# A fused attention and Fourier kernel on one Trainium2 core: most big loads past the thirteenth product issued by ScalarE in place of SyncE

## The chip, the core and the metric

The kernel runs on one core of a Trainium2 chip. The core has five engines that run their own instruction streams and wait for each other by semaphores: TensorE (PE, matrix products into PSUM banks), VectorE (DVE), ScalarE (ACT), GpSimd (POOL) and SyncE (SP, which computes nothing and here issues DMAs). Sixteen DMA engines move data between HBM and on-chip memory; an instruction on SP, ACT or POOL starts a transfer. The metric is device time in microseconds of one execution, lower is better.

## What is computed

Two independent parts, put side by side in the output. Part A is causal sliding-window attention with 32 heads of 32 columns and a window of 256; part B is a two-dimensional Fourier transform written as products with given matrices, of which the real part is kept.

```python
# A: x, wqkv, wo of 2048x1024, 1024x3072, 1024x1024
qkv = x @ wqkv
scores = einsum("bhqd,bhkd->bhqk", q, k) * (Dh ** -0.5)
scores = where((i - j >= 0) & (i - j < 256), scores, -1e9)
a = einsum("bhqk,bhkd->bhqd", softmax(scores), v) @ wo
# B: x of 2048x1024, matrices of 2048x2048 and 1024x1024
re, im = x @ dft_hid_re.T, x @ dft_hid_im.T
b = dft_seq_re @ re - dft_seq_im @ im
out = concatenate([a, b], axis=-1)
```

Everything is float32 in and out.

## The kernel before

**Products.** Each float32 operand is scaled and split into a high and a low float16 half (`split`, L129: ACT writes the high half, DVE the low one); three passes of float16 matmuls (`PASSES`, L48) replace one float32 product. The time runs through three stages.

*First stage* (L948 to L985, to about 560 us): 96 products of 24 matmuls with 512 columns each, listed in `order` (L409): q, k and v of eight head groups. The three PSUM banks of `bank` rotate; `qk_out` (L905) and L968 to L975 copy a finished bank by ACT (L907, L968) and DVE (L126, L969), and SP stores the result to the scratch tensors `qk` and `vs` in HBM. `tasks` (L414) ties other work to the number n of a product: loads, maxima or means (`top`, `mean`), scales and splits of later weights, and the preparation of part B: `xp_load` and `xp_step` (L631, L636) turn blocks of B's x into seven sums for a Strassen-like product and store them in `xs`; `wp_load` and `wp_step` (L668, L676) do so for the hidden-dimension matrices in the tile `wx` (views `praw(0)` to `praw(3)`).

*Rounds* (L1121 to L1202, to about 1540 us): 48 units in four rounds of 12. A round has four units of kind x (hidden transform) and eight of kind c (sequence transform). A unit is one call of `seven` (L1047): seven products of 12 matmuls, at positions 0 to 6, into the banks a, b, a, c, a, b, a. After position 0 ACT copies bank a into bank c (L1084), after positions 1, 2, 3 and 6 it copies a bank to an output tile (L1053), after 4 and 5 DVE adds (L1055). A bank is used again after one other product, so a copy has about one product's time. After each position, `hook(n, turn)` runs what `do(n, turn, ...)` noted for it: `u_load` loads the two float32 halves of a coming unit of kind c from `cs` into `raw_u` (five buffers `raw`), `u_top` takes their mean on ACT, `u_scale` makes the scale (a small product `pt_u` on PE), `u_step` splits them into `un_a`, `un_b`, `un_c`. For a unit of kind x, `x_left` loads these from `xs` instead.

*Attention* (`attention`, L218) is woven into both stages: `tick` (L382) advances it after every few matmuls by a rate. A block b has the scores of 128 queries for two heads (PE `s` and `far`), a mask copy and maximum (DVE), exponentials (ACT L278), a split (ACT L281, DVE L282), a transposing DMA on SP (L284) and two masks on POOL; six blocks later comes the product with v. `do_load` (L226) fetches q and k of four blocks into one of two `qk` buffers, three blocks ahead of use (L370) or, where the data isn't there yet, at use (L249).

*Last stage* (L1205 on): the product with wo.

**Order.** A scheduler places instructions on each engine from the program's order and its own estimate of times. `tc.issue_after(x)` only forbids a place ahead of x. Each engine runs its stream strictly in order. `behind_act[0]` is the last ACT copy of a bank. Tiles come from pools with a fixed number of buffers; a load into a buffer waits until its last reader is done. Each DMA on SP or ACT reports on one of eight completion semaphores, taken in turn, and waits for the DMA that used the same one before.

Before the change SP issues every transfer but the stores that accumulate (POOL, L1145): loads, transposes and stores stand in one stream.

Of the kernel before, what the change touches and what calls it, by code (L numbers as in the profile page):

```python
# [15 lines left out]
AF = mybir.ActivationFunctionType  # L16
# [29 lines left out]
HP = 8 * P  # L46
# [7 lines left out]
def fused_kernel(ctx: ExitStack, tc: tile.TileContext, xa, wqk, wv, wo, xb, wd, cs, out):  # L54
    nc = tc.nc
    PSUM = bass.MemoryType.PSUM

    qk = tc.dram_tile((NG, NCH, 3, DH, HG, 2, CH), F16, name="qk")
# [42 lines left out]
    nbank, units_on, stored, soon = [0], [], [], [True]  # L101
# [4 lines left out]

    def load_raw(src, shape, name, pool=None, tag="raw", **kw):
        r = (pool or rawp).tile([P] + shape, F32, tag=tag, name=f"raw_{name}", **kw)
        with tc.issue_after(stored[0].ins) if stored else nullcontext():
            nc.sync.dma_start(r, src)  # L110
        return r


# [31 lines left out]

    behind = []

    marks = []

    def top(key, raw, i, n):  # L150

        if i == 0:
            tops[key] = small.tile([P, n], F32, tag=f"top{n}", name=f"top_{key}")
        with tc.issue_after(behind[0].ins) if behind else nullcontext():
            vec(nc.vector.tensor_reduce, tops[key][:, i:i + 1], raw, axis=AX.XY, op=ALU.max,
                apply_absolute_value=True)

    def mean(key, raw, i, n):

# [58 lines left out]
    def attention():  # L218
# [4 lines left out]
        st, cur, q2s, k2s, vts, store_o = {}, {}, {}, {}, {}, []  # L223
        far = ps_s.tile([P, 2, 2, P], F32, tag="far", bufs=1, name="far")

        def do_load(g, hp, sc):  # L226
            if (g, hp, sc) in q2s:
                return
            u = att.tile([96, 2, 2, CH], F16, tag="qk", name=f"qk_{g}_{hp}_{sc}")
            nc.sync.dma_start(u.rearrange("p h a t -> p (h a t)"), qk[g, sc, :, :, 2 * hp:2 * hp + 2]  # L230
                              .rearrange("j d h a t -> (j d) (h a t)"))
            q2s[g, hp, sc], k2s[g, hp, sc] = u[:, :, 0], u[:, :, 1]

        def do_load_v(g, hp, sc):
# [8 lines left out]
        def s_step(b, j):  # L243
            g, hp, sc, i = blocks[b]
            qb = sc * QB + i
            nb = min(qb + 1, 3)
            if j == 0:
                if i == 0:
                    do_load(g, hp, sc)  # L249
                    do_load_v(g, hp, sc)  # L250
                st[b] = {"s": ps_s.tile([P, 2, 2 * P], F32, tag="s", name=f"s_{b}")}
                if nb == 3:
                    st[b]["far"] = far[:, b % 2]
            d = st[b]
            s = d["s"]
            edges = [k for k in range(qb + 1 - nb, qb + 2) if k in (qb + 1 - nb, qb - 1, qb + 1) or k % QB == 0]
            for k0, k1 in zip(edges, edges[1:]):
                at = (k0 - (qb - 1)) * P
                mm(d["far"][:, j] if at < 0 else s[:, j, at:at + (k1 - k0) * P],
                   q2s[g, hp, sc][:, j, i * P:i * P + P],  # L260
                   k2s[g, hp, k0 // QB][:, j, k0 % QB * P:k0 % QB * P + (k1 - k0) * P],
                   start=True, stop=True, skip_group_check=True)
            if j == 0:
                return
            w = min(nb, 2) * P
            sv = s[:, :, 2 * P - w:]
            nc.vector.copy_predicated(s[:, :, P:], upper2, d["far"] if nb == 3 else never2)  # L267
            mx = att.tile([P, 2], F32, tag="mn", bufs=6, name=f"mx_{b}")
            nc.vector.tensor_reduce(mx, sv, axis=AX.X, op=ALU.max, negate=True)  # L269
            bias = att.tile([P, 3], F32, tag="bias", bufs=6, name=f"bias_{b}")  # L270
            es = esc[g][:, sc:sc + 1]
            nc.scalar.activation(bias[:, :2], mx, AF.Identity, bias=pshift, scale=es)  # L272
            if b % 2 == 1:

                marks[:] = [nc.gpsimd.tensor_scalar(bias[:, 2:3], bias[:, 0:1], 1.0, None, op0=ALU.mult)]  # L275

            for h in range(2):
                nc.scalar.activation(sv[:, h], sv[:, h], AF.Exp, bias=bias[:, h:h + 1], scale=es)  # L278
            hl = att.tile([P, 8 * P], F16, tag="hl", bufs=3, name=f"hl_{b}")
            hi, lo = (hl[:, a * w:a * w + 2 * w].rearrange("p (h k) -> p h k", h=2) for a in (0, 2))  # L280
            nc.scalar.activation(hi, sv, AF.Copy)  # L281
            behind[:] = [nc.vector.tensor_tensor(lo, sv, hi, op=ALU.subtract)]  # L282
            t = att.tile([P, 8, P], F16, tag="t", bufs=6, name=f"t_{b}")
            line[:] = [nc.sync.dma_start_transpose(t[:, :4 * min(nb, 2)], hl[:, :4 * w])]  # L284
            d["t"] = t
# [66 lines left out]
        for b in range(nblk + LAG):  # L352
            for j in range(2):
                yield (blocks[b][0], blocks[b][2]) if b < nblk else None
                if b < nblk and j == 0:
                    s_step(b, 0)
                    s_step(b, 1)
                if j == 1 and b % 2 == 0 and b >= LAG:
                    v_step(b - LAG)
                    g, hp, sc, i = blocks[b - LAG + 1]  # L360
                    if i == QB - 1:
                        o_step(g, hp, sc)
                if j == 1 and b % 2 == ZAT and 3 <= b < nblk + 4:
                    for m in (b - 3 - (ZAT == 0), b - 2 - (ZAT == 0)):
                        if 0 <= m < nblk:
                            z_step(m)
                if j == 1 and store_o and (b >= nblk or blocks[b][3] == 3):
                    with tc.issue_after(line[0].ins):
                        nc.sync.dma_start(*store_o.pop(0))
                if j == 1 and b < nblk and blocks[b][3] == 1 and b + 3 < nblk:  # L370
                    g, hp, sc, _ = blocks[b + 3]
                    if (g, sc) in ready:
                        do_load(g, hp, sc)
                if j == 1 and b < nblk and blocks[b][3] == 3 and b + 1 < nblk:
                    g, hp, sc, _ = blocks[b + 1]
                    if (g, sc) in ready:
                        do_load_v(g, hp, sc)
# [78 lines left out]
    def praw(i):  # L456
        return cellx["wx"][:, i * 2048:(i + 1) * 2048].bitcast(F32)
# [106 lines left out]
    behind_act = []  # L564
# [66 lines left out]
    def xp_load(m):  # L631
        c, k = m // 4, m % 4
        for j, t in ((0, 8 * c + k + 4), (1, 8 * c + k)):
            nc.sync.dma_start(praw(m % 2 * 2 + j), xb[t].rearrange("p d t -> p (d t)"))

    def xp_step(n, m, step):  # L636
        r1, r2 = (praw(m % 2 * 2 + j).rearrange("p (d t) -> p d t", t=P) for j in range(2))
# [30 lines left out]
    def wp_load(p, k, blocks):  # L668
        for b in blocks:
            src = wd[p, 1 - b % 2, 2 * (b // 2) + k]  # L670
            if p == 1:
                nc.sync.dma_start(praw(b), src.rearrange("p d c -> p (d c)"))
            else:
                held[k, b] = load_raw(src, [2, CH], f"wd{k}_{b}")

# [97 lines left out]
    def u_load(n, j=0):  # L773
        if n < len(units):
            kind, p, c, i = units[n]
            raws[n, j] = rawp.tile([P, ND, P], F32, tag="raw", name=f"raw_u{n}_{j}")
            (load if i < 2 else nc.sync.dma_start)(raws[n, j], cs[p, 2 * i + j, :, 8 * c:8 * c + 8])

    def u_top(n, j):

# [17 lines left out]
    def x_left(n, step):  # L798

        _, _, c, k = units[n]  # L800
        src = xs[4 * c + k]
        u = uns.setdefault(n, {})
        part = lambda t, k0: (lambda h, d: t[:, h, k0 + d])
        if step == "t":
            t = spare[:, k % 2 * 8 * P:(k % 2 + 1) * 8 * P]
            nc.sync.dma_start(t, src[:, 6 * HP:])
            u[5] = part(t.rearrange("p (h k t) -> p h k t", h=2, k=4), 0)
            return
        j, held_by = {"a": (0, (0, 3)), "c": (1, (6, 4)), "b": (2, (2, 1))}[step]
        t = stp.tile([P, 2, ND, P], F16, tag="st", name=f"un{n}_{step}").rearrange("p h d t -> p (h d t)")  # L810
        nc.sync.dma_start(t, src[:, 2 * j * HP:2 * (j + 1) * HP])
        for k, pos in enumerate(held_by):
            u[pos] = part(t[:, k * HP:(k + 1) * HP].rearrange("p (h d t) -> p h d t", h=2, d=4), 0)

# [291 lines left out]
    with tc.tile_pool(name="pb", bufs=1) as pb:  # L1106
# [11 lines left out]
        def do(n, turn, f, *args):  # L1118
            todo.setdefault((n, turn), []).append((f, args))

        for r in range(4):  # L1121
# [7 lines left out]
                    do(n - 1, 0, x_left, n, "t")  # L1129
            for j in range(8):  # L1130
                n = c0 + j
                do(n - 3, 1, u_load, n, 1)
                do(n - 3, 5, u_load, n, 0)
                do(n - 2, 0, u_top, n, 1)
                do(n - 2, 2, u_top, n, 0)
                do(n - 2, 6, u_scale, n)
                for step, turn in enumerate((0, 1, 1, 2, 3, 4)):
                    do(n - 1, turn, u_step, n, step)
# [125 lines left out]
```

## Time and profile before

| What | Value |
|---|---|
| runs | 1696.62, 1700.10, 1697.67 us; median 1697.67 |
| profiled execution | 1697.51 us, span 1695.7 us |
| HBM read, written | 166.99 MB, 106.17 MB |
| hardware DMA queue q1 | 321.48 MB, 75.9% of 16 engines |
| granted TensorE clock | 1.000 |

The median issue-to-landing times of the loads that matter are 4.8 us (`raw_u` and `qk`), 4.8 to 5.5 us (`un_a`, `un_b`, `un_c`), 5.6 us (`raw_wd`), 5.9 us (`xb` into `wx`).

Rows of the timeline give the start and duration in us, the engine (SPq is SP's instruction stream, PEld PE's weight loads), the line of the kernel, the operation, output<-inputs by tile name, shapes and a count; in brackets, the engine's idle time ahead and what ended it. A row of waits gives who waited for whom: total us, times, longest us. Matmul ends are modelled, and adjacent matmuls overlap in the records.

### The profile page before, as it was taken

How to read it: one execution, taken by the hardware profiler on the slowest of the kernel's cores; microseconds unless marked ns; L12 is line 12 of the kernel's file. 1: busy time of each engine (PE TensorE's matmuls, PEld its weight loads, DVE VectorE, ACT ScalarE, POOL GpSimd, SP SyncE). 2: the span in 40 equal slices, each digit the busy share in tenths (PEclk: the TensorE clock that was granted, in tenths of full speed). 3: DMA queues.
4: the chain of work that ended last, by engine and by line, in shares of the span. 5: the costliest groups of instructions: out<-in, count | busy, mean ns of one | idle time of the engine just before them, and what ended most of it. 6: DMA issues, size and time to landing. Idle time of an engine off the chain costs nothing.

```text
span 1695.7 us, 30919 instructions
## 1 busy us (share of the span) xinstructions
PE 1687.6 (100%) x11007; PEld 846.6 (50%) x11007; DVE 1304.8 (77%) x2256; ACT 1169.8 (69%) x2035; POOL 571.0 (34%) x812
## 2 busy tenths in 40 slices
PE   9999999999999999999999999999999999999999
PEld 4444545554555554555554555545555545444444
DVE  7657888888888689887688896688886698687442
ACT  4476666677877687887687886687887688563322
POOL 0000222334434341444423475433565425411000
DMA  6678999999999994887998999986999977866431
GB/s 246 239 269 246 248 289 285 279 259 303 245 234 222 208 225 122 205 200 171 232 245 250 196 182 182 230 200 120 193 183 203 227 181 140 174 184 120 116 99 75
DMA packets 469898, 348.62 MB, mean 206 GB/s; under 512 B 376944, under 2 KB 409968, under 8 KB 468848
## 3 DMA queue, kind: packets, MB, share of 16 engines
q1 hardware_dynamic: 462064, 321.48, 75.9%
q0 software_dynamic: 7680, 25.17, 9.0%
q8 instruction: 86, 1.41, 0.3%
q14 instruction: 68, 0.56, 0.1%
HBM read 166.99 MB, written 106.17 MB: 161 GB/s over the span
## 4 chain that ended last, share of the span: by engine, by line
PE 83%; ACT 4%; DMA 4%; DVE 3%; issue 3%; POOL 2%; SPq 0%; POOLq 0%; ACTq 0%; DVEq 0%
PE p_a L119 23%; PE pv L119 12%; PE p_b L119 11%; PE pk L119 9%; PE pq L119 9%; PE p_c L119 6%; PE po_a L119 5%; PE s L119 3%; PE po_b L119 2%; PE far L119 1%; PE po_c L119 1%; DMA o<-ohl 1%; POOL z L296 1%; ACT s L278 1%; POOL t L298 1%
## 5 line engine op out<-in xcount | busy, mean ns | idle before, releaser
L278 ACT ACTIVATE s<-s,bias,escs 128x256 f32<-128x256 f32 (+1 forms) x512 | 270.1, 528 | 11.7
L296 POOL TENSOR_SCALAR_AFFINE_SELECT z<-t 128x512 f16<-128x512 f16 x224 | 183.1, 825 | 190.0 <-PE pv L119 167.2
L275 POOL TENSOR_SCALAR bias<-bias 128x1 f32<-128x1 f32 x128 | 53.5, 418 | 548.0 <-ACT bias L272 405.3
L272 ACT ACTIVATE bias<-mx,pshift,escs 128x2 f32<-128x2 f32 x256 | 98.4, 384 | 165.4 <-DVE mx L269 164.4
L282 DVE TENSOR_TENSOR hl<-s,hl 128x512 f16<-128x512 f32 (+1 forms) x256 | 169.8, 664 | 50.4 <-ACT hl L281 49.9
L119 PEld LDWEIGHTS <-reg 128*128 128x128 f16 x1344 | 128.7, 97 | 141.6
L298 POOL TENSOR_SCALAR_AFFINE_SELECT t<-t 128x512 f16<-128x512 f16 x224 | 188.1, 848 | 11.6
L119 PE MATMUL p_a<-reg,un_c 128*128 128x512 f16 x768 | 181.4, 379 | 0.5 <-DVE reg L859 0.3
L119 PE MATMUL pk<-reg,wu_k 128*128 128x512 f16 x768 | 174.3, 379 | 0.0
L269 DVE TENSOR_REDUCE mx<-s 128x2 f32<-128x512 f32 (+1 forms) x256 | 170.7, 667 | 3.4
L119 PE MATMUL pv<-reg,reg 128*128 128x512 f16 x768 | 172.5, 379 | 0.0
L119 PEld LDWEIGHTS <-un_c 128*128 128x128 f16 x1152 | 109.9, 97 | 121.8 <-issue 2.4
L119 PEld LDWEIGHTS <-un_b 128*128 128x128 f16 x1152 | 109.4, 97 | 117.4 <-issue 0.7
L119 PEld LDWEIGHTS <-un_a 128*128 128x128 f16 x1152 | 109.4, 97 | 116.5
L119 PE MATMUL pq<-reg,wu_q 128*128 128x512 f16 x696 | 156.3, 379 | 0.0
L281 ACT ACTIVATE hl<-s 128x512 f16<-128x512 f32 (+1 forms) x256 | 148.8, 581 | 5.5
L119 PE MATMUL p_a<-reg,un_b 128*128 128x512 f16 x576 | 136.4, 379 | 0.1
L119 PE MATMUL p_c<-reg,un_a 128*128 128x512 f16 x576 | 136.5, 379 | 0.0
L119 PE MATMUL p_b<-reg,un_b 128*128 128x512 f16 x576 | 136.3, 379 | 0.1
L119 PE MATMUL p_a<-reg,un_a 128*128 128x512 f16 x576 | 136.2, 379 | 0.0
L267 DVE COPY_PREDICATED s<-upper,far 128x256 f32<-128x256 uint32 x224 | 94.3, 421 | 51.6 <-PE s L119 50.6
L119 PEld LDWEIGHTS <-qk 96*128 96x128 f16 x1056 | 87.6, 97 | 63.6 <-DMA qk<-qk 2.2
(217 smaller groups left out, 3136.6 us busy)
## 6 DMA issues: line engine op xcount, KB each, us to landing
raw_u<-in_cs_dram SPq DMA_DIRECT2D x64, 512.0 KB, 4.8
qk<-qk SPq DMA_DIRECT2D x64, 384.0 KB, 4.8
out_dram<-y POOLq DMA_DIRECT2D x72, 256.0 KB, 6.2
raw_wd<-in_wd_dram SPq DMA_DIRECT2D x24, 512.0 KB, 5.6
vs<-yv SPq DMA_DIRECT2D x32, 264.0 KB, 4.1
vt<-vs SPq DMA_DIRECT2D x64, 132.0 KB, 3.5
qk<-yq SPq DMA_DIRECT2D x32, 256.0 KB, 4.0
raw_wo<-in_wo_dram SPq DMA_DIRECT2D x16, 512.0 KB, 8.6
```

The costliest lines, as they stand in the source:

```text
L119: fixed[:] = [nc.tensor.matmul(*args, **kwargs)]
L267: nc.vector.copy_predicated(s[:, :, P:], upper2, d["far"] if nb == 3 else never2)
L269: nc.vector.tensor_reduce(mx, sv, axis=AX.X, op=ALU.max, negate=True)
L272: nc.scalar.activation(bias[:, :2], mx, AF.Identity, bias=pshift, scale=es)
L275: marks[:] = [nc.gpsimd.tensor_scalar(bias[:, 2:3], bias[:, 0:1], 1.0, None, op0=ALU.mult)]
L278: nc.scalar.activation(sv[:, h], sv[:, h], AF.Exp, bias=bias[:, h:h + 1], scale=es)
L281: nc.scalar.activation(hi, sv, AF.Copy)
L282: behind[:] = [nc.vector.tensor_tensor(lo, sv, hi, op=ALU.subtract)]
L296: nc.gpsimd.affine_select(out=z, in_=pk, compare_op=ALU.is_gt, fill=0.0, base=0, pattern=[[0, 4], [-1, P]], channel_multiplier=1)
L298: nc.gpsimd.affine_select(out=pk, in_=pk, compare_op=ALU.is_ge, fill=0.0, base=0, pattern=[[0, 4], [1, P]], channel_multiplier=-1)
```

## The change

Loads issued by ACT get a helper, `bulk`, with a place behind the last copy of a bank by ACT. `load_raw` uses it once product 12 has been reached (`soon` is then False). So do the loads of `xb` and of `wd` into `wx`, `u_load` and `x_left`. The prefetch of `qk` three blocks ahead moves to ACT as well, with a place behind the exponentials of the block before the present one (`behind_exp`); the load at use stays on SP. `u_load` and `u_top` come one turn later. Transposes, stores, value tiles (`vt`), the loads of wo and of attention results for the last stage and the four `w_slot` loads to reg2 and three to wx stay on SP.

```diff
     def load_raw(src, shape, name, pool=None, tag="raw", **kw):
         r = (pool or rawp).tile([P] + shape, F32, tag=tag, name=f"raw_{name}", **kw)
-        with tc.issue_after(stored[0].ins) if stored else nullcontext():
-            nc.sync.dma_start(r, src)
+        if soon[0]:
+            with tc.issue_after(stored[0].ins) if stored else nullcontext():
+                nc.sync.dma_start(r, src)
+        else:
+            bulk(r, src)
         return r
...
-    marks = []
+    marks, behind_exp = [], []
...
+    def bulk(dst, src):
+        with tc.issue_after(behind_act[0].ins) if behind_act else nullcontext():
+            nc.scalar.dma_start(dst, src)
...
-        def do_load(g, hp, sc):
+        def do_load(g, hp, sc, queue=None):
...
-            nc.sync.dma_start(u.rearrange("p h a t -> p (h a t)"), qk[g, sc, :, :, 2 * hp:2 * hp + 2]
-                              .rearrange("j d h a t -> (j d) (h a t)"))
+            with tc.issue_after(behind_exp[0].ins) if queue else nullcontext():
+                (queue or nc.sync).dma_start(u.rearrange("p h a t -> p (h a t)"), qk[g, sc, :, :, 2 * hp:2 * hp + 2]
+                                             .rearrange("j d h a t -> (j d) (h a t)"))
...
-                nc.scalar.activation(sv[:, h], sv[:, h], AF.Exp, bias=bias[:, h:h + 1], scale=es)
+                e = nc.scalar.activation(sv[:, h], sv[:, h], AF.Exp, bias=bias[:, h:h + 1], scale=es)
+            behind_exp[:] = behind_exp[-1:] + [e]
...
                     if (g, sc) in ready:
-                        do_load(g, hp, sc)
+                        do_load(g, hp, sc, nc.scalar)
...
-            nc.sync.dma_start(praw(m % 2 * 2 + j), xb[t].rearrange("p d t -> p (d t)"))
+            bulk(praw(m % 2 * 2 + j), xb[t].rearrange("p d t -> p (d t)"))
...
             if p == 1:
-                nc.sync.dma_start(praw(b), src.rearrange("p d c -> p (d c)"))
+                bulk(praw(b), src.rearrange("p d c -> p (d c)"))
...
-            (load if i < 2 else nc.sync.dma_start)(raws[n, j], cs[p, 2 * i + j, :, 8 * c:8 * c + 8])
+            bulk(raws[n, j], cs[p, 2 * i + j, :, 8 * c:8 * c + 8])
...
-            nc.sync.dma_start(t, src[:, 6 * HP:])
+            bulk(t, src[:, 6 * HP:])
...
-        nc.sync.dma_start(t, src[:, 2 * j * HP:2 * (j + 1) * HP])
+        bulk(t, src[:, 2 * j * HP:2 * (j + 1) * HP])
...
-                do(n - 3, 1, u_load, n, 1)
-                do(n - 3, 5, u_load, n, 0)
-                do(n - 2, 0, u_top, n, 1)
-                do(n - 2, 2, u_top, n, 0)
+                do(n - 3, 2, u_load, n, 1)
+                do(n - 3, 6, u_load, n, 0)
+                do(n - 2, 1, u_top, n, 1)
+                do(n - 2, 3, u_top, n, 0)
```

SP's DMA rows fall from 1127 to 870 and ACT gets 257. Line numbers of the changed kernel are larger by 3 to 9 (L1053 becomes L1062, L786 becomes L795); all loads through `bulk` carry L163 there. PE keeps its instructions; only small products for scales (`pt`) move. Three places, in the built order:

SP before, in the first stage at product 67, ahead of the load `qk_1_1_0` (group 1, second pair of heads); `yq4_3` and `yk4_0` are results of products on their way to HBM:

```order
L284 DMA_TRANSPOSE t_44_4283<-hl_44_4280 128x8x128
L349 DMA_TRANSPOSE o_1_0_1_4155<-ohl_1_0_1_4322 128x4x128
L911 DMA qk_57<-yq4_3_4340 128x2x512
L912 DMA qk_57<-yq4_3_4340 128x512
L230 DMA qk_1_1_0_4395<-qk_57 96x2048
L912 DMA qk_57<-yk4_0_4422 128x512
```

ACT after the change, at the same place:

```order
L290 ACTIVATE hl_44_4280<-s_44_4266 128x512
L355 ACTIVATE ohl_1_0_1_4322<-o_1_0_1_4155 128x256
L916 ACTIVATE yq4_3_4340<-pq4_3_4257 128x512
L170 ACTIVATE junk_100,top_wq5_4345<-raw_wq5_4192 128x1024
L163 DMA wx_113<-in_wd_dram 128x1024 x2
L238 DMA qk_1_1_0_4395<-qk_57 96x2048
L280 ACTIVATE bias_45_4377<-mx_45_4375,pshift_95,escs_118 128x2
L286 ACTIVATE s_45_4369<-s_45_4369,bias_45_4377,escs_118 128x256 x2
```

The load no longer stands behind the two stores of `yq4_3`, but behind the ACT copy that makes `yq4_3`, a mean and two other loads, and ahead of block 45's exponentials.

SP before, in the rounds between units 20 and 21 (`t_169` to `t_173` are transposes of attention blocks, `raw_u23_0` a half of unit 23):

```order
L777 DMA raw_u23_0_12500<-in_cs_dram 128x1024
L284 DMA_TRANSPOSE t_169_12404<-hl_169_12401 128x8x128
L284 DMA_TRANSPOSE t_170_12443<-hl_170_12440 128x8x128
L284 DMA_TRANSPOSE t_171_12522<-hl_171_12519 128x8x128
L369 DMA ots_59<-o_5_0_0_12206 128x512
L240 DMA vt_5_0_3_12533<-vs_58 128x4x132
L284 DMA_TRANSPOSE t_172_12572<-hl_172_12569 128x8x128
L349 DMA_TRANSPOSE o_5_0_1_12459<-ohl_5_0_1_12622 128x4x128
L230 DMA qk_5_1_0_12684<-qk_57 96x2048
```

ACT after the change, from the last copy of unit 20 (`y1<-p2_20_a`) on:

```order
L1062 ACTIVATE y1_6683<-p2_20_a_12261,sc_u20_11939 128x512
L163 DMA raw_u23_0_12541<-in_cs_dram 128x1024
L280 ACTIVATE bias_171_12512<-mx_171_12510,pshift_95,escs_118 128x2
L286 ACTIVATE s_171_12504<-s_171_12504,bias_171_12512,escs_118 128x256 x2
L135 ACTIVATE un22_a_12579<-raw_u22_0_12258,sc_u22_12534 128x1024
L290 ACTIVATE hl_171_12517<-s_171_12504 128x512
L1093 ACTIVATE p2_21_c_12546<-p2_21_a_12544 128x512
```

The load now stands behind the copy of position 6. The mean of `raw_u23_1`, which stood there before, comes twelve rows later, behind the copy of position 1.

ACT before, in the first stage at the first products of v (`xp1` is the mean of two blocks of B's x in `wx`):

```order
L968 ACTIVATE yv0_1_1028<-pv0_1_1003,vf_105 128x16x32
L163 ACTIVATE junk_100,top_wo_551<-raw_wo_6_994 128x1024
L132 ACTIVATE wx_113<-wx_113,vxp_106 128x512
L968 ACTIVATE yv0_2_1071<-pv0_2_1046,vf_105 128x16x32
L163 ACTIVATE junk_100,top_xp1_1082<-wx_113 128x1024 x2
```

and after:

```order
L977 ACTIVATE yv0_1_1028<-pv0_1_1003,vf_105 128x16x32
L170 ACTIVATE junk_100,top_wo_551<-raw_wo_6_994 128x1024
L135 ACTIVATE wx_113<-wx_113,vxp_106 128x512
L163 DMA wx_113<-in_xb_dram 128x1024 x2
L977 ACTIVATE yv0_2_1071<-pv0_2_1046,vf_105 128x16x32
L163 DMA raw_wd1_0_1076<-in_wd_dram 128x1024
L170 ACTIVATE junk_100,top_xp1_1082<-wx_113 128x1024 x2
```

The two loads for `xp1` stand one bank copy ahead of the instruction that reads them; on SP they had been issued at 88.7 and 94.1 us, some 40 us ahead of it.

## Prediction

> **What bounds the kernel now.** I read the page's busy line first, then busy time by stretch, then the waits of TensorE. In the stretch table the columns are: stretch and length, then busy microseconds of PE, its weight loads, DVE, ACT and POOL with instruction counts, granted clock, DMA share and GB/s.
>
> ```profile
> span 1695.7 us, 30919 instructions
> PE 1687.6 (100%) x11007; PEld 846.6 (50%) x11007; DVE 1304.8 (77%) x2256; ACT 1169.8 (69%) x2035; POOL 571.0 (34%) x812
> ...
> 80.00:340.00 260.00, 260.00 (x1593) 128.22 (x1592) 199.32 (x384) 179.18 (x304) 54.60 (x85) 1.00 0.94 272
> 340.00:560.00 220.00, 218.48 (x1609) 114.00 (x1605) 182.78 (x321) 163.39 (x288) 90.03 (x128) 1.00 1.01 250
> 560.00:600.00 40.00, 39.62 (x308) 21.05 (x306) 28.53 (x49) 29.06 (x57) 16.37 (x26) 1.00 1.03 208
> 600.00:1130.00 530.00, 529.31 (x3792) 273.71 (x3791) 432.80 (x771) 417.20 (x767) 227.56 (x323) 1.00 0.91 205
> 1130.00:1500.00 370.00, 369.66 (x2507) 187.31 (x2506) 295.97 (x518) 277.14 (x490) 171.22 (x226) 1.00 0.89 183
> ```
>
> The change acts from about 77 us to 1500 us. Between 80 and 1500 us PE lacks 0 + 1.52 + 0.38 + 0.69 + 0.34 = 2.93 us. The clock is granted in full. "Busy" alone could deceive, since a record of a 512-column matmul overlaps the next; so I checked the spacing of starts.
>
> ```profile
> 880.94 2.75 PE L119 MATMUL p_b<-reg,un_b 128*128 128x512 f16 x12
> 883.15 0.55 ACT L1084 ACTIVATE p_c<-p_a 128x512 f32<-128x512 f32 x1
> 883.75 2.75 PE L119 MATMUL p_a<-reg,un_b 128*128 128x512 f16 x12
> ```
>
> Twelve matmuls whose modelled ends span 2.75 us are 2.59 us of work by their starts (the chain of waits writes the same groups as 2.59), 0.216 us each. The last record outlives its slot by 0.16 us, so a wait is up to 0.16 us longer than PE's idle time says. These are PE's waits after 5 us:
>
> ```profile
> PE s L119 <- DMA qk<-qk: 1.5, 1, 1.5
> ...
> PE p_a L119 <- ACT y L1053: 0.4, 1, 0.4
> PE p_a L119 <- DVE y L1055: 0.3, 1, 0.3
> PE p_a L119 <- DVE reg L859: 0.3, 1, 0.3
> PE p_a L119 <- ACT p_c L1084: 0.2, 1, 0.2
> ```
>
> Five waits: 2.93 + 5 x 0.16 = 3.7 us is all that the change can win, and it can win that only by doing everything right. 3.4 us (0.2%) is about what a measurement of this kernel can tell from no change. So the question is what the change can lose.
>
> **The change part by part.** It issues 257 loads from ACT instead of SP: 64 `raw_u`, 64 pieces from `xs`, 60 `qk`, 24 blocks from `xb` and `wd` into `wx`, 24 `raw_wd`, and 21 others (6 wo, 4 wv, 7 wk, 4 wq). What one issue takes, from the views of two source lines (min/median/max in ns):
>
> ```profile
> L777 SPq DMA_DIRECT2D raw_u<-in_cs_dram x48: 327/338/1226, 629.3 to 1487.9; - x48
> ...
> L230 SPq DMA_DIRECT2D qk<-qk x64: 319/498/1600, 122.6 to 1415.4; - x64
> ```
>
> At 0.34 to 0.50 us, 257 issues are some 110 us of SP's time that become ACT's. No row shows ACT issuing a DMA. Bounds: nothing, if ACT's sequencer issues while the engine still works; 0.45 us each, if the engine stands. The nearest rows lean to the first:
>
> ```profile
> 1007.57 0.60 ACT L281 ACTIVATE hl<-s 128x512 f16<-128x512 f32 x1
> 1008.06 0.68 ACT L1053 ACTIVATE y<-p_b,sc_u 128x512 f32<-128x512 f32 x1
> ```
>
> Each begins 0.11 us before the one ahead ends, so the sequencer is ahead of the engine, and a moved load mostly stands behind a copy of 0.6 to 0.7 us that can cover 0.34 to 0.50.
>
> *What an uncovered issue costs.* In the rounds ACT copies finished banks (L1084, L1053), and PE comes back to a bank one product later. At 883.15 + 0.55 = 883.70 the copy ends, 0.05 us before PE needs it; elsewhere there is 2.08 us:
>
> ```profile
> 1004.86 0.56 ACT L1084 ACTIVATE p_c<-p_a 128x512 f32<-128x512 f32 x1
> ...
> 1007.50 1.03 PE L119 MATMUL p_a<-reg,un_c 128*128 128x512 f16 x4
> ...
> 595.69 0.68 ACT L1053 ACTIVATE y<-p_a,fx 128x512 f32<-128x512 f32 x1
> ...
> 1497.35 0.58 ACT L1084 ACTIVATE p_c<-p_a 128x512 f32<-128x512 f32 x1
> ```
>
> Reading each such pair, 13 copies leave under 0.5 us (the first and last are the last two rows); their slack adds up to 2.4 us. A full 0.45 us in front of each costs 13 x 0.45 - 2.4 = 3.4 us, a covered one nothing. I take the middle, +1.7 us: cover is the rule, but not every issue stands ahead of a tight copy nor behind a long instruction.
>
> *What it wins.* The one large wait of PE:
>
> ```profile
> 393.92 1.05 ACT L163 ACTIVATE junk<-raw_wq 128x1024 uint8<-128x1024 f32 x1
> ...
> 404.30 0.39 SPq L230 DMA_DIRECT2D qk<-qk  x1
> ...
> 408.87 0.28 PE L119 MATMUL s<-qk 96*128 96x128 f16 x2 [1.52 <-DMA qk<-qk]
> ```
>
> The load stands on SP behind transposes and the stores of `yq4_3`. On ACT it stands behind the mean of `wq5`, which ends at 394.97. PE wanted it at 408.87 - 1.52 = 407.35; it takes 4.57 us from issue to first use, so anything ahead of 402.8 will do. -1.5 us. What is late next is the other qk load of that stretch, which no listed wait names.
>
> *Waits that move along.* SP had waited for buffers on behalf of these loads:
>
> ```profile
> SPq L777 <- DVE un_c L126: 33.4, 13, 4.1
> SPq L777 <- DVE un_b L126: 20.9, 13, 2.3
> SPq L811 <- PE s L119: 15.0, 12, 2.5
> SPq L806 <- PE p_b L119: 13.8, 9, 4.4
> ```
>
> If ACT waited for them, exponentials and bank copies would queue behind. But SP waited because it was early:
>
> ```profile
> 998.14 1.27 DVE L126 SCALAR_TENSOR_TENSOR un_b<-raw_u,sc_u,un_b 128x1024 f16<-128x1024 f32 x1
> ...
> 999.37 0.54 SPq L777 DMA_DIRECT2D raw_u<-in_cs_dram  x1
> ...
> 1001.46 0.69 ACT L1053 ACTIVATE y<-p_a,sc_u 128x512 f32<-128x512 f32 x1 [1.05 <-PE p_a L119]
> ```
>
> SP issues as DVE frees the buffer; the new place is behind the copy at 1001.46, 2 us after that. For `qk` it is the same: its buffer is freed by the scores of the block at hand, and the exponentials next in line on ACT need those scores too. New is that a load on ACT can stand for a DMA of SP: all loads, stores and transposes share eight completion semaphores in turn, and each waits for the one eight back. Eight back is some 12 us at about 1,130 DMAs in 1,696 us, against landings of 4 to 6 us. I cost these waits at nothing; uncovered, they are the second rival. Transposes and stores come sooner on SP, which has 257 rows fewer; PE waits for none of them, so nothing. POOL keeps its instructions, but for seven pairs of neighbours that change places.
>
> Sum: 1697.5 (profiled execution: span 1695.7 and 1.8 around it; the median is 1697.67) - 1.5 + 1.7 = **1697.7 us**, no change that can be told.
>
> **The rivals.** *Issue is held up by transposes (slower).* The large transposes alone keep SP issuing for 256 x 1.25 = 320 us, a fifth of the span, and an issue right behind one is long:
>
> ```profile
> L284 SPq DMA_TRANSPOSE t<-hl x256: 1188/1254/6185, 147.1 to 1453.5; - x128
> ...
> 1014.10 1.25 SPq L349 DMA_TRANSPOSE o<-ohl  x1
> 1015.45 1.60 SPq L230 DMA_DIRECT2D qk<-qk  x1
> ```
>
> If ACT's issues suffer the same, a fifth of some 170 in the rounds are 1.1 us longer than the median, which no 0.7 us copy covers. At one tight copy in five and 0.5 us each that is 34 x 0.2 x 0.5 = 3.4 us, with the 3.4 of the 13 places: 1697.5 - 1.5 + 6.8 = 1702.8. It decides the sign once more than about 5 us of ACT delay reach PE. Against it: the 1.60 can be a full queue of SP alone.
>
> *The waits come along (much slower).* The four rows are 83 us in 47 waits, 1.8 us each. ACT's idle time from 600 to 1500 us is 112.8 + 92.9 = 206 us; 83 of waits and 77 of issues would use 160 of it. If half of the waits meet a copy with 1 us of slack, 23 x 0.8 = 18 us: about 1716. The Trainium skill, page "DMA: Bandwidth & Descriptors", section "Anatomy of one DMA", says that DMA engines never wait for semaphores, the issuing sequencer does so ahead of dispatch; by that rule whatever is not yet free stops ACT. The rows above say that it is free.
>
> *Loads land late.* Issued where ACT stands, loads lose SP's head start. In the first stage the pair for `xp1` now stands behind the copy of `yv0_1` and a split, some 3.5 us ahead of its mean:
>
> ```profile
> wx<-in_xb_dram SPq DMA_DIRECT2D x16, 512.0 KB, 5.9
> ...
> 128.02 0.71 ACT L132 ACTIVATE wx<-wx,vxp 128x512 f16<-128x512 f32 x1
> 132.21 1.05 ACT L163 ACTIVATE junk<-wx 128x1024 uint8<-128x1024 f32 x1
> ```
>
> A landing time of 5.9 us makes ACT stand for about 2.4 us there, and at some dozen like places. A product takes 24 x 0.216 = 5.2 us and three banks rotate, so copies have 10 us and PE sees nothing unless stands add up: +4 us if they do at two or three places, 1701.5. The Trainium skill, page "DMA: Bandwidth & Descriptors", section "Queues, rings and completion order", has each DMA engine take turns between SP's row of queues and ACT's, packet by packet: loads would then share the engines with transposes that now stand behind them, and by that rule land later still. This profile has one hardware queue and shows neither.
>
> *All of PE's waits vanish (faster)*: 1697.5 - 3.7 = 1693.8.
>
> **How the numbers follow.** Forecast 0.60, transposes 0.17, late loads 0.10, waits along 0.06, faster 0.07. Faster by over 0.2% 0.07, within 0.60, slower 0.33. The range is 1694.2 to 1706.5: below it is most of the faster case, above it the waits-along case and the upper part of the first rival, together under 0.2. The likeliest case alone spans 1694.3 to 1701.
>
> **What would show it.** A second hardware queue on the page; no wait of PE for `qk` near 407; SP's waits on `un_b` and `un_c` gone and no ACT wait of their size in their place. Right: PE's waits for L1084 and L1053 together under 4 us. Wrong: those rows at 5 us and more with issues of over 1 us on ACT ahead of the copies (first rival), ACT issues that wait for DVE or PE (second), or ACT's means waiting for DMA with PE idle before 350 us (third).

## The result and the profile after

| | before | after |
|---|---|---|
| median of 4 runs | 1698.88 us (1696.62 to 1704.37) | 1812.63 us (1786.46 to 1834.74) |
| profiled execution | 1697.51 us, span 1695.7 | 1786.46 us, span 1784.7 |
| ratio to before | 1 | 1.0554, 95% interval 1.0467 to 1.0641 |

The change makes the kernel about 5.5% slower. The runs of the changed kernel spread over 2.7%; the ratio is that of the runs within 1.5% of the fastest on either side, so it lies below the ratio of the medians, and the profile is of the fastest run, so it shows the least of the damage.

The page of the changed kernel first: the busy line of PE and the DMA queues (packets, MB, share of 16 engines).

```profile
span 1784.7 us, 30812 instructions
...
PE 1710.0 (96%) x11007; PEld 850.3 (48%) x11007; DVE 1301.5 (73%) x2256; ACT 1170.4 (66%) x2035; POOL 557.9 (31%) x812
...
q1 hardware_dynamic: 426976, 198.78, 54.5%
q10 hardware_dynamic: 35088, 122.70, 25.4%
```

ACT and DVE have no more work than before (ACT 1170.4 against 1169.8 us, DVE 1301.5 against 1304.8), and the same 321.48 MB are moved, but 122.70 MB of them go through a second hardware queue, q10. PE has the same 11007 instructions; its records last 22 us longer in all, and it is idle for 75 - 8 = 67 us more. Busy time by stretch, columns as in the prediction:

```profile
80.00:340.00 260.00, 247.66 (x1475) 120.22 (x1474) 178.62 (x342) 167.67 (x284) 46.49 (x75) 0.99 0.92 241
340.00:560.00 220.00, 203.04 (x1443) 103.80 (x1442) 171.29 (x311) 147.86 (x260) 81.44 (x113) 0.98 1.10 247
...
600.00:1130.00 530.00, 511.84 (x3644) 262.98 (x3642) 413.25 (x736) 399.71 (x732) 209.52 (x308) 0.99 0.97 193
1130.00:1500.00 370.00, 348.03 (x2383) 176.56 (x2382) 282.37 (x490) 266.21 (x484) 150.69 (x211) 0.98 0.95 173
```

PE lacks 12.3, 17.0, 18.2 and 22.0 us in stretches where it lacked 0, 1.5, 0.7 and 0.3, and the clock is no longer granted in full. What PE waits for (total us, times, longest):

```profile
PE far L122 <- DVE s L275: 22.0, 14, 3.8
PE p_a L122 <- ACT p_c L1093: 16.2, 6, 10.2
PE p_a L122 <- ACT y L1062: 7.2, 9, 2.0
PE pv L122 <- DVE yv L978: 4.3, 2, 3.2
PE pv L122 <- POOL z L305: 4.0, 2, 3.4
PE p_b L122 <- DMA un_b<-xs: 3.1, 1, 3.1
...
PE s L122 <- DMA qk<-qk: 0.7, 1, 0.7
```

Hardly any of it is for a load. PE waits for DVE's mask copies and ACT's bank copies, so ACT and DVE are late. DVE waits for ACT in its turn, most of all for ACT's write of the high half into `hl`, here after the change and then before it.

```profile
DVE hl L291 <- ACT hl L290: 116.5, 66, 12.7
```

```profile
DVE hl L282 <- ACT hl L281: 49.9, 56, 2.7
```

Why ACT is late is seen in the source lines that issue on ACT, and in the transposes of the tile `hl` (issue times in ns, min/median/max; then who waited for it, us and times):

```profile
L163 ACTq DMA_DIRECT2D raw_u<-in_cs_dram x64: 334/335/394, 633.0 to 1581.4; - x64
...
L238 ACTq DMA_DIRECT2D qk<-qk x60: 310/333/411, 216.3 to 1504.2; - x60
```

```profile
L293 SPq DMA_TRANSPOSE t<-hl x256: 1194/1443/11602, 148.4 to 1540.3; - x128
...
  POOL z L305: 111.1, 31
  ACT hl L290: 40.1, 12
  ACT s L286: 14.9, 2
...
DMA to landing us min/median/max: 3.0/6.2/26.0
```

The same view of the kernel before ends:

```profile
  POOL z L296: 22.5, 11
  ACT yk L907: 1.8, 1
...
DMA to landing us min/median/max: 2.4/4.6/13.0
```

Issuing on ACT is cheap, 0.33 us at the median and never over 0.42 in these two rows; of all 257 loads one takes more than 1 us to issue (1.45 us). The transposes, which the change does not touch, are what became slow: from 4.6 to 6.2 us at the median, from 13.0 to 26.0 at most, and by my count of the trace 47 of 256 land after more than 10 us where 2 did. They meet more loads the longer they take: in the changed kernel's trace a transpose (of `hl` or `ohl`) lands after 3.66 us (median of 35) when no load of ACT overlaps it, 4.49 with one (79), 6.08 with two (82), 8.38 with three (59), 11.15 with five (23). This alone does not say which is the cause, since a transpose that is late for any reason overlaps more loads; the experiments have to.

The largest hole, as the timeline has it: SP first, then ACT, then PE.

```profile
1378.28 19.38 SPq L293 DMA_TRANSPOSE t<-hl  x3
...
1386.14 0.33 ACTq L163 DMA_DIRECT2D un_a<-xs  x1
1386.72 0.38 ACT L280 ACTIVATE bias<-mx,pshift,escs 128x2 f32<-128x2 f32 x1
1399.85 0.33 ACTq L163 DMA_DIRECT2D reg<-xs  x1
1400.23 1.11 ACT L286 ACTIVATE s<-s,bias,escs 128x256 f32<-128x256 f32 x2 [13.13 <-DMA t<-hl]
1401.37 0.60 ACT L290 ACTIVATE hl<-s 128x512 f16<-128x512 f32 x1
1401.86 0.59 ACT L1093 ACTIVATE p_c<-p_a 128x512 f32<-128x512 f32 x1
...
1402.51 1.44 PE L122 MATMUL p_a<-reg,un_b 128*128 128x512 f16 x3 [10.23 <-ACT p_c L1093]
```

Loads of `un_a`, `un_b`, `un_c` are in flight and three transposes take 19.4 us to issue. The next load in ACT's order, `reg<-xs`, takes its turn on a completion semaphore that a transpose used last; it stands until that transpose lands, 12.8 us. Exponentials and the bank copy L1093 stand behind it, and PE stands for the copy. The price does not end there (stretch, length, busy PE to POOL, granted clock):

```profile
1393.00:1402.00 9.00, 0.00 (x0) 0.00 (x0) 0.00 (x1) 1.71 (x4) 1.86 (x3) 0.65 1.14 236
1402.50:1405.50 3.00, 3.00 (x8) 1.04 (x8) 1.22 (x3) 2.03 (x5) 1.91 (x4) 0.50 0.87 197
1406.00:1409.40 3.40, 3.40 (x20) 1.67 (x19) 1.81 (x3) 1.14 (x3) 1.53 (x3) 1.00 1.02 155
```

After the hole PE runs at half its clock for another 3 us: 8 matmuls of 512 columns, where at 0.216 us each 13 would fit. Over the whole trace the clock is halved for 41 us, in seven pieces behind holes. Taking PE's spacing of starts against that of before, 48 holes of over 0.3 us make 77.8 us and 74 matmuls at half clock another 14.6. With the 4.6 us of before taken off that is 87.8 of the 89 us between the two spans.

### The profile page after: what moved, and what is told of

Read it like the earlier page. It is cut to its first block, busy times and chain, and to the rows that moved or that the text cites. A ratio compares the mean times of both kernels' runs of the same rounds, so it can differ in the third digit from the quotient of the medians.

```text
span 1784.7 us, 30812 instructions
## 1 busy us (share of the span) xinstructions
PE 1710.0 (96%) x11007; PEld 850.3 (48%) x11007; DVE 1301.5 (73%) x2256; ACT 1170.4 (66%) x2035; POOL 557.9 (31%) x812
## 3 DMA queue, kind: packets, MB, share of 16 engines
q10 hardware_dynamic: 35088, 122.70, 25.4%
q0 software_dynamic: 7680, 25.17, 9.2%
## 4 chain that ended last, share of the span: by engine, by line
PE 61%; DMA 16%; DVE 9%; ACT 8%; issue 4%; POOL 1%; SPq 1%; ACTq 0%; DVEq 0%; POOLq 0%
PE p_a L122 18%; PE pq L122 9%; PE p_b L122 9%; DMA t<-hl 7%; PE pv L122 6%; PE p_c L122 5%; PE po_a L122 4%; PE pk L122 4%; PE po_b L122 2%; ACT s L286 2%; PE s L122 2%; DMA xs<-wx 2%; DMA wx<-in_xb_dram 1%; PE po_c L122 1%; DMA raw_wd<-in_wd_dram 1%
## 5 line engine op out<-in xcount | busy, mean ns | idle before, releaser
L305 POOL TENSOR_SCALAR_AFFINE_SELECT z<-t 128x512 f16<-128x512 f16 x224 | 176.9, 797 | 233.3 <-PE pv L122 111.3
L283 POOL TENSOR_SCALAR bias<-bias 128x1 f32<-128x1 f32 x128 | 45.7, 357 | 591.5 <-ACT bias L280 419.4
L290 ACT ACTIVATE hl<-s 128x512 f16<-128x512 f32 (+1 forms) x256 | 148.7, 582 | 50.0 <-DMA t<-hl 40.1
L122 PE MATMUL pv<-reg,reg 128*128 128x512 f16 x768 | 176.1, 384 | 4.3 <-DVE yv L978 4.3
L122 PE MATMUL p_a<-reg,un_b 128*128 128x512 f16 x576 | 140.6, 387 | 16.2 <-ACT p_c L1093 14.9
```

Of the source, the lines that this page charges most:

```text
L122: fixed[:] = [nc.tensor.matmul(*args, **kwargs)]
L305: nc.gpsimd.affine_select(out=z, in_=pk, compare_op=ALU.is_gt, fill=0.0, base=0, pattern=[[0, 4], [-1, P]], channel_multiplier=1)
```

## The experiments

Three theories were set against each other. **Turns**: two hardware queues share the DMA engines, and transposes on SP's queue land late behind loads of ACT's. **Standing**: ACT, strictly in order, stands at its loads for shared semaphores and for their issue. **Late places**: the loads are asked for too late, whoever asks. Differences in us below are of medians, to the runs of before beside them.

**The same places, issued by SP.**

```diff
-            nc.scalar.dma_start(dst, src)
+            nc.sync.dma_start(dst, src)
...
-                        do_load(g, hp, sc, nc.scalar)
+                        do_load(g, hp, sc, nc.sync)
```

> The changed kernel with its 257 loads at the same places of the program (behind the last bank copy or the exponentials, means one turn later), but issued by SP again: one hardware queue. Turns theory (two hardware queues share the DMA engines packet by packet, so that transposes on SP's queue land late behind loads of ACT's queue, and hold ACT and POOL): the loss goes, 1696 to 1706 us, landing of t<-hl at 4.6 us median and 13 at most. Standing theory (ACT, strictly in order, stands at its loads for completion semaphores that it shares with SP): the loss goes too, same range. Late-places theory (the loads are asked for too late, whichever engine asks): the loss stays, 1770 us and above.

1706.97 us against 1699.44, ratio 1.0047 (1.0029 to 1.0065). The landing of its `t<-hl`:

```profile
DMA to landing us min/median/max: 2.4/4.9/11.6
```

The places cost 7.5 us, 1 us above the range of turns and standing; the rest of the loss needs another queue or another issuer. Late places falls as the main cause.

**ACT issues, but moves nothing.** The kernel before, and beside each of the 257 loads:

```diff
+    def tiny(after=None):
+        after = behind_act if after is None else after
+        ntiny[0] += 1
+        with tc.issue_after(after[0].ins) if after else nullcontext():
+            nc.scalar.dma_start(tinies[ntiny[0] % 16], cs[0, 0, :1, 0])
```

> The kernel before, with all loads on SP, and beside each of the 257 loads a copy of 512 bytes from HBM to HBM that ACT issues at the place where the change puts the load. These take completion semaphores in turn with SP's transfers, and ACT must issue them in order, but they move next to nothing. Turns theory: no traffic on the second queue, so 1696 to 1703 us, t<-hl landing at 4.6 us median. Standing theory (shared semaphores and issue): most of the loss stays, 1760 us and above, with ACT's copies waiting several us for transposes. Late-places theory: 1696 to 1703.

1711.03 us, ratio 1.0066 (1.0046 to 1.0086): 11.6 us, above the range of turns and far below that of standing. In its trace ACT stands for 24.5 us, 16 times, at one of these copies whose semaphore a transfer of SP used last. So standing is real, and with the issue itself, and with transposes that land as before (4.6 us at the median), it is worth an eighth of the loss (11.6 of 94 us). What standing costs when the transposes are late, this run does not show.

**Smaller packets.** The changed kernel, with rows of 4 KB cut in HBM to rows of 1 KB; the control is the kernel before with the same layout.

```diff
-    xs = tc.dram_tile((8, P, 7 * HP), F16, name="xs")
+    xs = tc.dram_tile((8, 14, P, HP // 2), F16, name="xs")
...
-            nc.scalar.dma_start(dst, src)
+            nc.scalar.dma_start(cut(dst), rows(src))
...
+    wqk, wv, wo, xb, wd, cs = (cut(m) for m in (wqk, wv, wo, xb, wd, cs))
```

> The changed kernel with the inputs (all but xa) and the scratch tensor xs laid out in HBM so that a row of 4 KB becomes four of 1 KB: loads move the same bytes from the same places on ACT, in packets of 1 KB in place of 4 KB (qk loads keep 4 KB). Turns theory: a 256-byte packet of a transpose waits for one packet of the other queue per turn; 64 of them per DMA engine, behind packets of about 46 ns in place of about 160 ns, wait some 3 us and not up to 10: t<-hl landing at most 15 us in place of 26, and at least half of the loss goes, 1700 to 1745 us. Standing and late-places theories: packet size means nothing or costs a little, 1780 us and above.

> Control: the kernel before, all on SP, with the same HBM layout in rows of 1 KB. All theories: 1696 to 1706 us; if it is slower than that, the difference is the price of smaller packets and is taken off the run with small packets on ACT.

The control: 1706.24 us, ratio 1.0036 (1.0022 to 1.0051). With ACT's loads: 1769.88 us (1749.62 to 1787.67), ratio 1.0320 (1.0275 to 1.0365). Less the control's 0.36%, about half of the 5.54% is left, so packet size matters, which standing and late places do not explain. But the time is above the range given, and in the one profile, of a run of 1787.67 us, a transpose still takes 24.1 us to land, 37 of 256 take more than 10 us, and the median landing is 6.1 us, against 6.2. The most direct measure is the rate of the transposes' 256-byte packets, counted in the trace in slices of 0.5 us between 90 and 1500 us:

| kernel | second queue still, packets per us | second queue moving |
|---|---|---|
| changed, rows of 4 KB | 655 | 250 |
| rows of 1 KB | 674 | 299 |
| rows of 512 bytes (below) | 675 | 364 |

The levels depend on which slices are counted, the order less so: over all slices that lie between two with transposes, the rates are 535, 520 and 541 with the second queue still and 214, 245 and 306 with it moving.

**Rows of 512 bytes, and the changed kernel again.**

> As the run with rows of 1 KB, but with rows of 512 bytes. If the queues take turns by packets, the transposes get a still larger share: their rate while the second queue is moving rises well over the 299 packets per us of the run with 1 KB (250 with 4 KB), and the time falls to 1715 to 1750 us. If the share is not by packets, the rate stays near 300 and the time at 1750 to 1790 us, or rises, as smaller packets take more time of the DMA engines for the same bytes.

> The changed kernel once more, on the same chip as the two others: 1785 to 1835 us by all theories, t<-hl landing at a median of about 6.2 us. It says whether single profiles of it can be compared with those of the variants.

With 512 bytes 1765.18 us (1761.09 to 1784.24), ratio 1.0412 (1.0354 to 1.0470); the changed kernel again 1820.48 us (1803.63 to 1834.38). The rate rose as turns by packets has it, and the longest landing fell to 15.0 us. The time is not below that of 1 KB and lies in the range given for the other case; the median landing is 6.3 us, and 30 transposes still take more than 10 us. The second queue's share of the DMA engines also rose, from 25.4 to 28.6%, and rows of 512 bytes have no control on one queue. So smaller packets take some of the loss away, and the runs don't settle how much of it; that the queues take turns by packets agrees with the rates and is not shown by the times.

**One part of the loads at a time.** All three keep the places of the change; the parts not named are issued by SP.

> The changed kernel in which only the 69 loads of the first stage (weights, scans, blocks of xb and wd) are issued by ACT; the 128 loads of the rounds and the 60 qk prefetches go back to SP, at the same places. Turns theory: the loss comes where loads of the second queue meet transposes, so PE's holes lie before 560 us, t<-hl lands late there alone (over 10 us at most a dozen times after 560), 1725 to 1745 us. Standing theory (each issue on ACT costs, about 94 us over 257 loads): 69 loads cost some 25 us, 1732 us, but t<-hl lands no later than before.

> The changed kernel in which only the 128 loads of the rounds (raw_u, pieces of xs) are issued by ACT, the others by SP at the same places. Turns theory: PE's holes lie after 560 us, t<-hl lands late there (median over 5.5 us in the rounds), 1725 to 1750 us. Standing theory: 128 of 257 loads, some 47 us, 1754 us, with t<-hl landing as before.

> The changed kernel in which only the 60 qk prefetches are issued by ACT, the others by SP at the same places. Turns theory: a single load of 384 KB at a time adds at most about 1 us to a transpose, so 1703 to 1712 us, hardly more than with all loads on SP at these places (1707.0). Standing theory: 60 loads of 257, some 22 us on top of 1707, 1729 us.

| loads on ACT | median us | ratio | PE's loss, first stage / later | transposes over 10 us, first stage / later |
|---|---|---|---|---|
| none (same places) | 1706.97 | 1.0047 | 2.0 / 14.1 | 0 / 3 |
| 60 qk | 1711.05 | 1.0063 (1.0046 to 1.0079) | 1.2 / 17.1 | 1 / 12 |
| 69 of the first stage | 1743.85 | 1.0226 (1.0159 to 1.0293) | 45.5 / 21.1 | 14 / 6 |
| 128 of the rounds | 1737.16 | 1.0205 (1.0172 to 1.0238) | 2.5 / 38.0 | 0 / 20 |
| all 257 | 1812.63 | 1.0554 | 39.7 / 55.5 | 17 / 30 |

PE's loss is again from the spacing of its starts, in us. The landing of `t<-hl` from 90 to 560 us, first with the first stage's loads on ACT, then with those of the rounds:

```profile
DMA to landing us min/median/max: 3.1/6.6/18.3
```

```profile
DMA to landing us min/median/max: 2.4/4.9/9.0
```

Transposes are late mostly where big loads are on the other queue, and PE's loss moves with them. The three times lie within the ranges of turns. The 60 `qk` loads, some 22 us apart, go with 13 late transposes (3 with all loads on SP) and cost 9.9 us, 2.4 more than the 7.5 of the same places on SP, where standing gave them 22. (The profile with the first stage's loads on ACT is of a run of 1758.53 us, 15 us above the median, so its 45.5 can't be read as more than the 39.7 of all loads.)

**Another issuer, another queue.** The changed kernel with `nc.gpsimd.dma_start` in place of `nc.scalar.dma_start` in `bulk` and for `qk`.

> The changed kernel with its 257 loads issued by GpSimd, through its software queue, at the same places: the traffic is again on another queue than the transposes, but ACT issues nothing, and GpSimd's transfers have completion semaphores of their own. Turns theory: t<-hl lands late as in the changed kernel (median over 5.5 us, over 10 us some 30 to 60 times), and PE loses 40 to 100 us: 1740 to 1800 us, with ACT waiting for t<-hl by its hl buffers. Standing theory (the loss is ACT standing for shared semaphores): ACT never stands, t<-hl lands at 4.6 us median, 1700 to 1720 us. What GpSimd's own issue (about 1 us each) costs its masks comes on top in both and shows as PE or POOL waits for z.

1800.52 us, ratio 1.0568 (1.0508 to 1.0628), half a microsecond above the range of turns: as large a loss with nothing issued by ACT. Its queue line (25.17 MB of it are POOL's accumulating stores, as before the change), and who waited for `t<-hl`:

```profile
q0 software_dynamic: 41744, 147.87, 34.1%
```

```profile
  POOL z L305: 135.4, 38
  ACT hl L290: 72.1, 25
...
DMA to landing us min/median/max: 2.5/6.2/22.8
```

The transposes land as late as with ACT's queue, and ACT waits for its `hl` buffers instead of at loads. That a second queue makes transposes late, whoever feeds it, is shown. How much of this run's loss comes from them is not: POOL stands at its own loads for some 275 us, mostly until a buffer is free. PE waits only 4.3 us for POOL's `z`, but 23.7 us for DVE's scales (`top_u`, `scw`, `sc_u`), which loads that POOL issued late can explain as well.

**More hl buffers in the first stage.**

```diff
-            hl = att.tile([P, 8 * P], F16, tag="hl", bufs=3, name=f"hl_{b}")
+            if b % 5 > 2 and more[0]:
+                hl = more[0].tile([P, 8 * P], F16, tag="hl", name=f"hl_{b}")
+            else:
+                hl = att.tile([P, 8 * P], F16, tag="hl", bufs=3, name=f"hl_{b}")
```

> The changed kernel with five hl buffers in place of three in the first stage (two more in a pool that closes ahead of the rounds), all 257 loads on ACT. If transposes that land late reach PE because they hold hl buffers, ACT's waits for t<-hl before 560 us go to nearly nothing and 10 to 20 us of the first stage's loss with them: 1775 to 1800 us. If they reach PE in another way (semaphores that ACT's loads stand for, masks on POOL), nothing changes: 1785 to 1835 us as the changed kernel has it.

1813.23 us (1795.01 to 1822.71), ratio 1.0627: no gain. The extra buffers were in the wrong stage. ACT's waits for DMAs in the changed kernel, from 90 to 590 us and from 600 to 1540 us:

```profile
ACT junk L170 <- DMA wx<-in_xb_dram: 8.0, 6, 3.2
ACT bias L280 <- DMA xs<-wx: 7.8, 1, 7.8
...
ACT hl L290 <- DMA t<-hl: 4.8, 2, 4.3
ACT bias L280 <- DMA t<-hl: 4.4, 1, 4.4
```

```profile
ACT hl L290 <- DMA t<-hl: 35.3, 10, 11.4
ACT s L286 <- DMA t<-hl: 14.9, 2, 13.1
```

In the first stage only 4.8 us are waits for a buffer; there ACT stands for late loads (8.0 in the first row) and at loads whose semaphore a store or transpose holds (the rows for `bias`). In the rounds, where 35.3 us are buffer waits, more buffers weren't tried.

**Fewer hl buffers without a second queue.** The kernel before with `bufs=2` for `hl`.

> The kernel before, all loads on SP, with two hl buffers in place of three. In it a buffer is held from ACT's copy to the landing of its transpose for 7.1 us (median; 10.2 at the ninth tenth), two blocks take 9.5 us and three 14.0; in the changed kernel it is held for 8.8 us (15.4 at the ninth tenth) against three blocks of 14.7. If late transposes reach PE through hl buffers, shortening the room does without a second queue what longer holding does with it: ACT waits for t<-hl some 50 times, 1710 to 1740 us, with t<-hl landing no later than 4.6 us median. If hl buffers are not the path, 1697 to 1703 us.

1732.26 us against 1701.70, ratio 1.0195 (1.0150 to 1.0239). Its waits of ACT, and its landing:

```profile
ACT hl L281 <- DMA t<-hl: 57.4, 30, 5.4
```

```profile
DMA to landing us min/median/max: 2.4/4.5/12.7
```

Within the range, with 30 waits in place of the 50 expected: holding a buffer too long for the room there is costs 30 us by itself, with transposes on time and one queue. In the changed kernel a buffer is held for 8.8 us at the median and 15.4 at the ninth tenth, with three blocks taking 14.7, so the same path is open in the rounds, where the 35.3 us above lie; how much of the loss goes through it is not measured.

No version beat the kernel before; with PE lacking 2.93 us there, none that keeps PE's instructions could by more than the prediction's 3.7.

## Why the prediction was wrong

*The bound.* Nothing speaks against it: it gave 3.7 us as all that could be won, and no version is faster.

*Issue on ACT.* Right in kind: 0.33 us, and one issue in 257 over 1 us, so the first rival (issue held up by transposes) did not happen. The +1.7 us can't be judged by itself: 257 tiny issues cost 11.6 together with the semaphores that the prediction priced apart, at nothing, and for which ACT stands 24.5 us in that run.

*The qk wait.* The row at 407 went, and another `qk` wait of 0.7 us came. Its 1.5 us is lost in the rest.

*Buffers.* Right: ACT stands 5.0 us, 5 times, at loads for a buffer. The second rival in the form it was given, buffers not yet free, did not happen.

*Shared semaphores.* "Eight back is some 12 us ... against landings of 4 to 6 us. I cost these waits at nothing": this failed. ACT stands 35.6 us, 12 times, at loads whose semaphore a transfer of SP used last (20.1 of it for transposes). The landings of 4 to 6 us were medians of the kernel before; the change itself altered them, and their longest, 13.0 us, was already beyond 12.

*Transposes.* This is the step that failed most: "Transposes and stores come sooner on SP, which has 257 rows fewer; PE waits for none of them, so nothing." They are issued more slowly (1.44 us at the median, 1.25 before) and land later (6.2 us, 4.6 before), and that PE waits for none of them says nothing of who waits in between: ACT for `hl` buffers (40.1 us, none before), POOL for its masks (111.1 us, 22.5 before), ACT's loads for semaphores. The term put at nothing is most of the loss: with the same loads at the same places on SP's queue, 7.5 us of it are left.

*The third rival* had the rule in hand, that the engines take turns between SP's and ACT's queues, and asked only what it does to the loads. In the rounds most land up to 1 us later than before, at 5.2 us (`raw_u`), 5.7 (`qk`) and 4.5 to 6.4 (`un`), the short pieces `reg<-xs` 2.8 us later, at 6.8; in the first stage `raw_wd` lands at 7.5 us (5.6 before) and the blocks of `wd` in `wx` at 8.9 (5.6 before). ACT's means wait 8.0 us for the loads of `xb`, so this rival came true in part, and what it cost PE is not shown. The larger cost is on the other side: a transpose of 1024 packets of 256 bytes takes 1.6 us at 655 packets per us and 4.1 at the 250 that it has beside a queue of 4 KB rows. The Trainium skill, page "DMA: Bandwidth & Descriptors", section "Queues, rings and completion order", lets an engine drain a whole packet of typically 9 to 17 descriptors from one row before it turns to the next; the rates of the table, which rise as the other queue's rows shrink, agree with such turns and don't show their length.

*What stays open.* How the first stage's 40 us divide between standing at semaphores, late loads and late stores. The places cost 7.5 us and issue with semaphores 11.6; if these add up, the remaining 75 or so of 94 us (the ratio of 1.0554 on 1699) came only with big transfers on a second queue. How they divide between ACT's standing at semaphores of late transposes, held `hl` buffers and late loads stays open in the rounds too.

## What to carry to other kernels

Big loads on a queue of their own can delay latency-bound transfers of small packets (here transposes) on the other: with the loads at the same places, the transposes landed after 4.9 us at the median and 11.6 at most on one queue, after 6.2 and 26.0 on two. Before moving transfers to another queue, look for the transfer in the kernel whose landing sets a buffer's return, compare its holding time (7.1 us, ninth tenth 10.2) with the room that its buffers give (three blocks, 14.0 us), and price the move by that slack and not by the issue time saved. And an engine that finishes work for the critical one should not be given instructions that wait for other engines' transfers.

## What the runs showed of the hardware

- With a second queue moving 4 KB rows, transposes pass 250 packets of 256 bytes per us in place of 655, while all queues together move about as much (237 GB/s, against 210 in the slices of the same trace in which the second queue is still). What is lost is not bandwidth but the transposes' share of it.
- GpSimd's software queue does the same to transposes of SP's queue as ACT's hardware queue (landing 6.2 us at the median in both).
- A hole of 10 us on PE halves its clock for some 3 us after it; 0.50 was granted for 41 us in all in the profile above, and for 20.5 us in the run with two `hl` buffers on one queue. The Trainium skill, page "TensorE: Matmul & The Clock Gate", section "Part 1: The HAM clock gate (the "warmup" mystery)", gives half the clock after an idle window of about 3.4 us and until a busy one; the trace agrees, with pieces of 3.4, 6.8 and 10.2 us, though the piece at 337.6 us follows holes of only 1.7 and 1.1 us.
